# Splitting weights two tiles at a time, and the keys of two heads in one step

## The chip, the cores and the metric

One NeuronCore of a Trainium2 chip runs the whole program. The metric is the device time of one execution in microseconds (us), the median of several runs. Its engines are TensorE (PE, with its weight loads listed as PEld), VectorE (DVE), ScalarE (ACT), GpSimd (POOL) and SyncE (SP), which here only issues DMAs. Each engine works through its own queue in order; semaphores order them among each other.

## What is computed

Three stages follow each other on 4 batches of 576 tokens (2304 in all):

```python
scores = 0.125 * q @ k.T                       # 8 heads of 64, per batch
kth    = 32nd largest score of each row
attn   = softmax(where(scores >= kth, scores, -1e9))
x = (attn @ v), heads side by side             # 2304 x 512
h = x @ w_in                                   # 512 x 2048
y = where(h > 0, h, exp(min(h, 0)) - 1) @ w_out   # 2048 x 512
z = ((y @ w1) * (y @ w2)) @ w3 @ w_out2        # 512 x 1024 twice, 1024 x 1024, 1024 x 512
```

Inputs are float32 in the reference. The kernel gets the weights as 64-bit words.

## The kernel before

**Number formats.** Float32 precision is reached on fast matmuls by splitting each operand into a high half and a low half: a float16 tile `hi` holds the rounded value, `lo` the rest, and a product is hi\*hi + hi\*lo + lo\*hi (three matmuls). Both halves of a weight tile lie in one 128x512 float32 slot: `hi(t)` is its first 512 float16 columns, `lo(t)` the last 512. The weights are 48 such tiles: `Win`, `Wout` and `W12` with 16 each; `W34`, with 8 more, holds the product w3 @ w4, computed on the chip.

**Weight preparation.** For each of w_in, w_out, w1 and w2, `load64` (line 616) loads a 512 KB block of 64-bit words and merges the two 32-bit halves into a float32 tile (L633 ACT, L634 DVE, L635 ACT, L636 POOL). These staged tiles don't have slots of their own: `home` (line 643) places staged tile i in the final slot of tile i + 4 (w_in, w_out) or i + 2 (w1 and w2, together `w12`), and the last ones in slots of `W34` or in `PP`. When all 16 are there, `norm` finds a scale (Gram matmuls L394, DVE reductions), and `convert` (line 655) splits tile by tile: it writes `hi(W[i])` and `lo(W[i])` over the slot in which an earlier staged tile lay. So tile i can be split only after tile i - 4 (w_in, w_out) or i - 2 (w12).

`convert` takes the high half on ACT (L660, a copy to float16 with the scale as a per-partition operand). The low half is made in one of several modes, given by `PAR["cd"]` and `conv_modes`:

- "S": GpSimd scales the staged tile in place (L669) and subtracts the high half (L670). Six tiles of w_in, six of w_out and eight of w12; those of w12 are the odd tiles.
- "D": DVE does both in one instruction (L663). The eight even tiles of w12.
- "P": PE multiplies the staged tile by a scaled identity and subtracts the high half (L675, L676) into a psY bank, and DVE copies the bank out (L679). Ten tiles each of w_in and w_out.

**Keys.** `att_loads` (line 439) loads the keys of one batch and one pair of heads when they are first needed, 16 times in all. For each of the two heads, one DMA fills one of two raw buffers (a ring of two, shared with the values), ACT copies 128x576 to the rounded form (L450), and GpSimd replaces partitions 64 to 127 by the rest (L451). Keys needed again later come back from DRAM.

**Attention.** A step is 128 query rows of two heads: query split (L510 ACT, L511 POOL), QK into the bank psS (L529), evacuation by ACT (L531), eight-at-a-time top-32 on DVE (MAX8 L539, MATCH_REPLACE8 L541, four rounds per head), masking and exponential (L554, L556 ACT), split (L564 ACT, L565 POOL), transposing DMA, the product with the values (L582), normalization on DVE and split (L602 ACT, L603 POOL), and a transposing DMA (L604) into the chunk's activations X. A chunk is 256 tokens, 8 steps; there are nine.

**The rest of a chunk** on PE: units A (x @ w_in, L841 to L843), O (@ w_out, L878 to L880), B (@ w1 and @ w2, L920 to L922) and D (@ W34, L955 to L957), with the evacuations between them on ACT, DVE and GpSimd.

**Order of work.** Nothing is issued in program order. Each operation is recorded with an engine, an estimated cost, the keys it reads and writes and a priority; `Program.emit` (line 232) then simulates the queues forward and backward with these costs and issues the operations in the resulting order, which is fixed from then on. The priority holds an offset from the table `OFF` per kind of work and engine, and a term for the length of the chain behind the operation.

The lines that the change touches most directly:

```python
op("ACT", 613, lambda: A.activation(hi(W[i]), st, AF.Copy, scale=s), [*skeys, sk], [(nm, i)], pr)      # L660
op("POOL", 660, lambda: G.tensor_scalar(st, st, s, 1.0, op0=OP.mult, op1=OP.mult), [sk], skeys, pr)    # L669
op("POOL", 1160, lambda: G.tensor_tensor(lo(W[i]), st, hi(W[i]), op=OP.subtract), ...)                 # L670
```

Of the kernel before, what the change touches and what calls it, by code (L numbers as in the profile page):

```python
# [32 lines left out]
PAR = dict(rings=(2, 3, 4, 3, 1, 2, 5, 3), nxs=3, nxf=2, nxt=3, slack=1.6, fb=2, snake=1, blag=0, hv={}, lv={'wi': 16, 'wo': 16}, whole=(), cd={'wi': [0, 0, 6], 'wo': [0, 0, 6], 'w34': [0, 0, 8], 'w12': [8, 0, 8]}, pv=-577.81, pi=702.591, p34=-453.754, po=123.714, p12=822.408,   # L33
# [5 lines left out]
OFF = {":DVE": 16163, "A0:ACT": -38685, "A0:DVE": -4543, "A0:PE": 21441, "A0:POOL": 23849, "A1:ACT": 1589, "A1:PE": -13628, "A1:POOL": -11110,  # L39
# [214 lines left out]
def kernel(ctx: ExitStack, tc: tile.TileContext, qd, kd, vd, vn, w_in, w_out, w1, w2, w3t, w4, out,  # L254
                                   chunks=CHUNKS):
    nc = tc.nc
    w_in, w_out, w1, w2, w3t, w4 = [a.bitcast(I32) for a in (w_in, w_out, w1, w2, w3t, w4)]
    P = Program()
    CONV = {k: conv_modes(8 if k == "w34" else 16, *v) for k, v in PAR["cd"].items()}
    op = P.op  # L260
    NTL = sum(chunks)

# [11 lines left out]
    def slots(name, n):  # L274
        t = pool.tile([128, n, 512], F32, name=name)
        return t, [t[:, i] for i in range(n)]

    _, Win = slots("win", 16)
    WoutT, Wout = slots("wout", 16)
    W12T, W12 = slots("w12", 16)  # L280
    W34T, W34 = slots("w34", 8)
# [435 lines left out]
    def prep_in(pr):  # L717
        P.tag = "w_in"
        st = []
# [372 lines left out]
```

## Time and profile before

| | us |
|---|---|
| median of 3 runs (lowest to highest) | 1037.14 (1036.56 to 1039.12) |
| the profiled execution, its own time | 1037.07 |
| its span in the profile | 1035.3 |
| PE busy in the span | 955.4 |
| DVE busy | 870.8 |
| ACT busy | 819.4 |
| POOL busy | 739.7 |

Busy time counts the instructions of an engine, without its waits. Instructions of one engine overlap at their ends: an instruction begins before the one ahead of it has ended, so the spacing of starts is shorter than a duration. In the views, an instruction is named by its line, its engine, its operation and output<-input by the program's names; w is a tile of `W12` or `W34`, win and wout those of `Win` and `Wout`.

### The profile page before, as it was taken

Reading aid. Unit: us, or ns where it says so; the run is one execution under the profiler, and the core shown is the slowest. Engines: PE = TensorE matmul, PEld = TensorE weight load, DVE = VectorE, ACT = ScalarE, POOL = GpSimd, SP = SyncE. Lnnn points to the kernel's source line nnn. Section 1 sums busy time; section 2 is a strip of 40 time slices with the busy share of each in tenths; the row PEclk is TensorE's granted clock in tenths of the full one; section 3 lists DMA queues with packets and bytes.
Section 4 is the critical chain, followed back from the end, with each engine's and each line's share of the span. In section 5 each row is a group of like instructions: output and inputs, shape, how many; then the busy total and the mean of one; then the engine's idle time right before and its main releaser. Section 6 shows DMA issues by size and latency. Waiting matters only on the chain.

```text
span 1035.3 us, 24518 instructions
## 1 busy us (share of the span) xinstructions
PE 955.4 (92%) x9096; PEld 770.4 (74%) x9096; DVE 870.8 (84%) x1941; ACT 819.4 (79%) x1517; POOL 739.7 (71%) x795
## 2 busy tenths in 40 slices
PE   2466999896899999999999999999999999999998
PEld 2333455796788878878878897788789889878875
DVE  6999999999999999997999999575999999951010
ACT  6999977998999977976987798587778878944512
POOL 6999966799999846965985597479368657944701
PEclk9897999999999999999999999999999999999999
DMA  9987995867456774555476354524553353330000
GB/s 366 329 273 232 276 251 122 232 197 154 135 126 160 169 137 86 121 136 148 127 175 155 86 121 116 146 57 136 124 132 69 70 114 82 57 91 14 1 22 21
DMA packets 246744, 144.04 MB, mean 139 GB/s; under 512 B 195680, under 2 KB 222304, under 8 KB 246624
## 3 DMA queue, kind: packets, MB, share of 16 engines
q1 hardware_dynamic: 246624, 142.48, 54.1%
q8 instruction: 71, 1.16, 0.5%
q14 instruction: 49, 0.40, 0.1%
HBM read 80.65 MB, written 14.59 MB: 92 GB/s over the span
## 4 chain that ended last, share of the span: by engine, by line
DVE 36%; PE 26%; ACT 15%; POOL 7%; issue 7%; DMA 6%; DVEq 0%; POOLq 0%; ACTq 0%
DVE m L539 16%; DVE wk L541 14%; PE psY L783 3%; PE psR L920 2%; PE psR L921 2%; PE psR L922 2%; DMA pt<-pi 2%; PE psS L529 2%; DMA pp<-w 2%; PE psA L582 2%; ACT s L554 1%; PE psR L841 1%; PE psR L842 1%; PE psR L843 1%; ACT s L531 1%
## 5 line engine op out<-in xcount | busy, mean ns | idle before, releaser
L539 DVE MAX8 m<-wk 128x8 f32<-128x576 f32 x432 | 312.2, 747 | 0.8
L565 POOL TENSOR_TENSOR pi<-s,pi 128x576 f16<-128x576 f32 x144 | 185.5, 1296 | 78.8 <-ACT pi L564 67.7
L541 DVE MATCH_REPLACE8 wk<-m,wk 128x576 f32<-128x576 f32 x288 | 212.5, 741 | 0.0
L920 PE MATMUL psR<-x,w 128*128 128x256 f16 x576 | 157.3, 273 | 3.7 <-DVE t L940 3.7
L841 PE MATMUL psR<-x,win 128*128 128x256 f16 x576 | 157.8, 274 | 0.8 <-DVE t L940 0.5
L843 PE MATMUL psR<-x,win 128*128 128x256 f16 x576 | 157.4, 273 | 0.0
L842 PE MATMUL psR<-x,win 128*128 128x256 f16 x576 | 157.4, 273 | 0.0
L922 PE MATMUL psR<-x,w 128*128 128x256 f16 x576 | 157.0, 273 | 0.5 <-POOL w L670 0.5
L878 PE MATMUL psY<-g,wout 128*128 128x256 f16 x576 | 157.3, 273 | 0.0
L880 PE MATMUL psY<-g,wout 128*128 128x256 f16 x576 | 157.0, 273 | 0.0
L879 PE MATMUL psY<-g,wout 128*128 128x256 f16 x576 | 157.0, 273 | 0.0
L921 PE MATMUL psR<-x,w 128*128 128x256 f16 x576 | 157.0, 273 | 0.0
L554 ACT ACTIVATE s<-s,m 128x576 f32<-128x576 f32 x144 | 110.3, 776 | 40.8 <-DVE m L539 39.2
L529 PE MATMUL psS<-kt,qh 128*128 128x288 f32 x320 | 112.4, 366 | 31.4 <-ACT s L531 24.9
L531 ACT ACTIVATE s<-psS 128x576 f32<-128x576 f32 (+1 forms) x160 | 103.1, 644 | 17.0 <-PE psS L529 11.2
L556 ACT ACTIVATE s<-s,ty 128x576 f32<-128x576 f32 x144 | 107.4, 771 | 3.8 <-POOL ty L550 3.7
L539 DVE MAX8 m<-s 128x8 f32<-128x576 f32 x144 | 106.1, 746 | 3.9 <-ACT s L531 3.4
L541 DVE MATCH_REPLACE8 wk<-m,s 128x576 f32<-128x576 f32 x144 | 106.3, 741 | 0.0
L564 ACT ACTIVATE pi<-s 128x576 f16<-128x576 f32 x144 | 96.5, 679 | 9.4 <-DMA pt<-pi 9.1
L529 PEld LDWEIGHTS psS<-kt,qh 128*128 128x128 f32 x320 | 62.3, 195 | 44.9 <-ACT s L531 20.0
L529 PE MATMUL psS<-kt,ql 128*128 128x288 f32 x320 | 91.5, 300 | 1.0 <-POOL ql L511 1.0
L582 PEld LDWEIGHTS <-pt 128*128 128x128 f16 (+1 forms) x2240 | 77.8, 101 | 17.7 <-issue 8.0
(168 smaller groups left out, 2393.4 us busy)
## 6 DMA issues: line engine op xcount, KB each, us to landing
qr<-qd SPq DMA_DIRECT2D x72, 128.0 KB, 2.7
raw<-kd SPq DMA_DIRECT2D x32, 288.0 KB, 3.3
w<-w_in SPq DMA_DIRECT2D x16, 512.0 KB, 7.5
w<-w_out SPq DMA_DIRECT2D x16, 512.0 KB, 6.0
w<-w3t SPq DMA_DIRECT2D x16, 512.0 KB, 4.8
kd<-kt SPq DMA_DIRECT2D x12, 576.0 KB, 4.0
kt<-kd SPq DMA_DIRECT2D x12, 576.0 KB, 3.9
w<-w SPq DMA_DIRECT2D x12, 512.0 KB, 4.7
```

The lines of the kernel that those rows point to most:

```text
L529: T.matmul(psS[:, half, 0:288], lhsT=L[qs][:, hh], rhs=KT[kk][:, hh, half * 288:half * 288 + 288], start=li == 0, stop=li == 1)
L539: op("DVE", 665, lambda r=r, src=src, m8=m8, hh=hh: V.max(m8[:, hh, 8 * r:8 * r + 8], src), [skey], [mk], p1 + PAR["ot"] * STEP)
L541: op("DVE", 727, lambda r=r, src=src, w=w, m8=m8, hh=hh: V.match_replace(w, m8[:, hh, 8 * r:8 * r + 8], src, -3.0e38), [skey, mk], [k], p1 ...
L565: op("POOL", 1240, lambda Y=Y, PIs=PIs, hh=hh: G.tensor_tensor(PIs[:, hh, S:2 * S], Y[:, hh], PIs[:, hh, 0:S], op=OP.subtract), hks, [pk], ...
L841: T.matmul(o, lhsT=hi(W)[:, cs], rhs=X[:, 0, kd_, 0:N], start=kd_ == 0, stop=False)
L842: T.matmul(o, lhsT=hi(W)[:, cs], rhs=X[:, 1, kd_, 0:N], start=False, stop=False)
L843: T.matmul(o, lhsT=lo(W)[:, cs], rhs=X[:, 0, kd_, 0:N], start=False, stop=kd_ == 3)
L878: T.matmul(o, lhsT=hi(W)[:, cs], rhs=rh, start=ft == 0 and m % 2 == 0, stop=False, skip_group_check=True)
L879: T.matmul(o, lhsT=hi(W)[:, cs], rhs=rl, start=False, stop=False, skip_group_check=True)
L920: T.matmul(o, lhsT=hi(W)[:, cs], rhs=X[:, 0, kd_, 0:N], start=kd_ == 0, stop=False)
L921: T.matmul(o, lhsT=hi(W)[:, cs], rhs=X[:, 1, kd_, 0:N], start=False, stop=False)
L922: T.matmul(o, lhsT=lo(W)[:, cs], rhs=X[:, 0, kd_, 0:N], start=False, stop=kd_ == 3)
```

## The change

The high halves of w_in, w_out, w1 and w2 are made for two neighbouring tiles by one ACT instruction of 128x(2x512). Where the pair's mode is "S", one GpSimd instruction scales both tiles and one subtracts both. Modes "P" and "D" still work tile by tile, after the common high half. Modes are given per pair now, with the same number of tiles in each: w_in and w_out have three "S" pairs and five "P" pairs each, w12 four "D" pairs and four "S" pairs in turn. For keys, both raw buffers are loaded, then one ACT instruction copies both heads and one GpSimd instruction subtracts both. The estimated costs follow. All entries of `OFF` have new values.

```diff
-PAR = dict(... cd={'wi': [0, 0, 6], 'wo': [0, 0, 6], 'w34': [0, 0, 8], 'w12': [8, 0, 8]}, ...
+PAR = dict(... cd={'wi': [0, 0, 3], 'wo': [0, 0, 3], 'w34': [0, 0, 8], 'w12': [4, 0, 4]}, ...
-OFF = {":DVE": 16163, "A0:ACT": -38685, "A0:DVE": -4543, "A0:PE": 21441, "A0:POOL": 23849, "A1:ACT": 1589, ...
+OFF = {":DVE": 17176, "A0:ACT": -44777, "A0:DVE": -8789, "A0:PE": 18968, "A0:POOL": 19901, "A1:ACT": -5916, ...
...
-    CONV = {k: conv_modes(8 if k == "w34" else 16, *v) for k, v in PAR["cd"].items()}
+    CONV = {k: conv_modes(8, *v) for k, v in PAR["cd"].items()}
...
         for hh in range(2):
-            rs = nxt("raw", 2)
-            kr = raw[rs][:, 0:S]
-            dma(kr, kd[b, 2 * p + hh], 128 * S * 4, [], [("raw", rs)], pr)
-            op("ACT", 574, lambda kr=kr, hh=hh: A.activation(KT[ks][:, hh], kr, AF.Copy), [("raw", rs)], [("k", ks)], pr)
-            op("POOL", 1370, lambda kr=kr, hh=hh: G.tensor_tensor(KT[ks][64:128, hh], kr[64:128], KT[ks][64:128, hh].bitcast(F32), op=OP.subtract),
-               [("raw", rs)], [("k", ks)], pr)
+            dma(raw[nxt("raw", 2)][:, 0:S], kd[b, 2 * p + hh], 128 * S * 4, [], [("raw", hh)], pr)
+        rks, kr = [("raw", 0), ("raw", 1)], RAWT[:, :, 0:S]
+        op("ACT", 66 + 508 * 2, lambda: A.activation(KT[ks], kr, AF.Copy), rks, [("k", ks)], pr)
+        op("POOL", 143 + 1220 * 2, lambda: G.tensor_tensor(KT[ks][64:128], kr[64:128], KT[ks][64:128].bitcast(F32), op=OP.subtract), rks, [("k", ks)], pr)
...
+    def pair(WT, nm, i):
+
+        k = len(HOMES[nm])
+        if i < 16 - k:
+            return WT[:, i + k:i + k + 2]
+        return PP[:, 4:8].rearrange("p (a c) b -> p a (c b)", a=2) if nm == "w12" else W34T[:, i - 12 + 4 * (nm == "wo"):][:, 0:2]
+
+    def convert2(W, WT, nm, i, st, s, sk, pr, sid, kind="y"):
+
+        d2, ks = pair(WT, nm, i), [st[i][1], st[i + 1][1]]
+        keys = ks[0] + ks[1]
+        f2 = WT[:, i:i + 2].bitcast(F16)
+        h2, l2 = f2[:, :, 0:512], f2[:, :, 512:1024]
+        op("ACT", 66 + 547 * 2, lambda: A.activation(h2, d2, AF.Copy, scale=s), [*keys, sk], [(nm, i), (nm, i + 1)], pr)
+        if CONV[nm][i // 2] == "S":
+            op("POOL", 86 + 574 * 2, lambda: G.tensor_scalar(d2, d2, s, 1.0, op0=OP.mult, op1=OP.mult), [sk], keys, pr)
+            op("POOL", 80 + 1045 * 2, lambda: G.tensor_tensor(l2, d2, h2, op=OP.subtract), [*keys, (nm, i), (nm, i + 1)], [(nm, i, "l"), (nm, i + 1, "l")], pr)
+            return
+        for h in range(2):
+            rest(W, nm, i + h, st[i + h][0], ks[h], s, sk, pr, sid, kind, CONV[nm][i // 2])
+
     def convert(W, nm, i, st, skeys, s, sk, pr, sid, kind="y"):
...
-        mode = CONV[nm][i]
+        rest(W, nm, i, st, skeys, s, sk, pr, sid, kind, CONV[nm][i])
+
+    def rest(W, nm, i, st, skeys, s, sk, pr, sid, kind, mode):
...
-        for i in range(16):
+        for i in range(0, 16, 2):
             P.tag = "w_in.c"
-            convert(Win, "wi", i, st[i][0], st[i][1], scal("sin"), ("sc", "ni"), pr + PAR["ci"] * STEP, 0)
+            convert2(Win, WinT, "wi", i, st, scal("sin"), ("sc", "ni"), pr + PAR["ci"] * STEP, 0)
...
-        return [lambda i=i: convert(W12, "w12", i, st[i][0], st[i][1], scal(("s1", "s2")[i // 4 % 2]), ("sc", ("n1", "n2")[i // 4 % 2]), pr + PAR["c12"] * STEP, i // 4 % 2 * 2, "rot")
-                for i in range(16)]
+        return [lambda i=i: convert2(W12, W12T, "w12", i, st, scal(("s1", "s2")[i // 4 % 2]), ("sc", ("n1", "n2")[i // 4 % 2]), pr + PAR["c12"] * STEP, i // 4 % 2 * 2, "rot")
+                for i in range(0, 16, 2)]
```

`prep_out` changes as `prep_in` does. `rest` holds the modes' code of `convert`, unchanged.

## Rows read from the trace of the kernel before

**Rows 1.** The page's busy table: engine, busy us (share of the span), instructions.
```profile
PE 955.4 (92%) x9096; PEld 770.4 (74%) x9096; DVE 870.8 (84%) x1941; ACT 819.4 (79%) x1517; POOL 739.7 (71%) x795
```

**Rows 2.** Busy time by stage: stretch, length, each engine's busy us (instructions), PE clock, DMA.
```profile
core 0: us, PE busy (x) PEld busy (x) DVE busy (x) ACT busy (x) POOL busy (x), PEclk, DMA share, GB/s
46.00:107.00 61.00, 41.41 (x210) 20.68 (x210) 57.32 (x116) 59.91 (x106) 59.59 (x56) 0.84 0.83 265
107.00:183.00 76.00, 72.97 (x415) 40.49 (x415) 74.14 (x160) 63.63 (x122) 54.13 (x60) 0.98 0.90 213
183.00:243.00 60.00, 54.75 (x584) 48.44 (x581) 58.38 (x137) 56.21 (x103) 53.20 (x53) 0.97 0.83 214
243.00:300.00 57.00, 45.22 (x498) 39.42 (x495) 55.34 (x131) 53.03 (x99) 56.26 (x59) 0.97 0.53 127
300.00:912.00 612.00, 605.74 (x6285) 515.45 (x6283) 571.68 (x1280) 505.30 (x953) 440.06 (x490) 1.00 0.51 119
```

**Rows 3.** The timeline of PE at two joints: start us, length us, instructions.
```profile
106.75 0.38 PE L676 MATMUL psY<-wout,nident 128*128 128x512 f16 x1
107.28 1.96 PE L783 MATMUL psY<-w,pp 128*128 128x512 f32 x4
...
183.07 0.27 PE L841 MATMUL psR<-x,win 128*128 128x256 f16 x1
```

**Rows 4.** The activations X from 170 to 184 us: transposing DMAs, first and last start.
```profile
L604 SPq DMA_TRANSPOSE x<-xt x2: 1167/1167/1167, 171.0 to 180.8; - x2
...
DMA to landing us min/median/max: 2.3/3.7/5.1
```

**Rows 5.** The timeline of ACT: start us, length us, instructions (xN: several merged).
```profile
72.21 0.68 ACT L450 ACTIVATE kt<-raw 128x576 fp32r<-128x576 f32 x1
72.78 0.64 ACT L531 ACTIVATE s<-psS 128x576 f32<-128x576 f32 x1
...
85.98 2.54 ACT L660 ACTIVATE wout<-wout,sc 128x512 f16<-128x512 f32 x4
```

**Rows 6.** ACT copies by line: duration ns min/median/max, first to last start us.
```profile
L602 ACT ACTIVATE xt<-xf x72: 292/306/348, 85.2 to 940.3; 128x128 f16<-128x128 f32 x72
...
L450 ACT ACTIVATE kt<-raw x32: 665/682/741, 4.1 to 720.4; 128x576 fp32r<-128x576 f32 x32
...
L660 ACT ACTIVATE w<-w,sc x21: 705/712/742, 225.2 to 320.6; 128x512 f16<-128x512 f32 x21
```

**Rows 7.** High halves (L660 alone) in the two stages: ACT busy us (instructions).
```profile
46.00:107.00 61.00, 20.91 (x31) 0.84 0.83 265
243.00:300.00 57.00, 13.85 (x20) 0.97 0.53 127
```

**Rows 8.** The timeline of GpSimd, as rows 5.
```profile
88.11 2.28 POOL L670 TENSOR_TENSOR wout<-wout 128x512 f16<-128x512 f32 x2
...
94.76 1.41 POOL L451 TENSOR_TENSOR kt<-raw,kt 64x576 fp32r<-64x576 f32 x1
96.25 1.29 POOL L636 TENSOR_TENSOR w<-w 128x512 int32<-128x512 int32 x1
```

**Rows 9.** GpSimd instructions by line, as rows 6.
```profile
L603 POOL TENSOR_TENSOR xt<-xf,xt x72: 416/429/1013, 120.4 to 941.4; 128x128 f16<-128x128 f32 x72
...
L669 POOL TENSOR_SCALAR w<-w,sc x16: 684/692/1126, 103.7 to 332.5; 128x512 f32<-128x512 f32 x16
...
L670 POOL TENSOR_TENSOR w<-w x14: 1152/1159/1618, 245.0 to 333.3; 128x512 f16<-128x512 f32 x14
```

**Rows 10.** GpSimd's subtractions for weights (L670 alone) in the two stages, as rows 7.
```profile
46.00:107.00 61.00, 12.02 (x10) 0.84 0.83 265
243.00:300.00 57.00, 15.40 (x13) 0.97 0.53 127
```

**Rows 11.** GpSimd's subtractions for keys (L451 alone) in the two stages, as rows 7.
```profile
46.00:107.00 61.00, 7.05 (x5) 0.84 0.83 265
243.00:300.00 57.00, 6.00 (x4) 0.97 0.53 127
```

**Rows 12.** Waits of PE, 243 to 300 us: in total, times, longest.
```profile
PE psS L529 <- ACT s L531: 7.5, 5, 2.8
```

**Rows 13.** DVE instructions with two SBUF inputs by line, as rows 6.
```profile
L663 DVE SCALAR_TENSOR_TENSOR w<-w,sc x7: 725/761/1198, 245.8 to 279.6; 128x512 f16<-128x512 f32 x7
...
L477 DVE SCALAR_TENSOR_TENSOR vv<-raw,sc,vv x16: 870/1412/1933, 38.2 to 710.9; 128x640 f16<-128x640 f32 x16
```

**Rows 14.** High halves of w12 and the last subtraction: first and last start us.
```profile
L660 ACT ACTIVATE w<-w,sc x17: 705/711/742, 242.9 to 278.3; 128x512 f16<-128x512 f32 x17
...
L670 POOL TENSOR_TENSOR w<-pp,w x1: 1163/1163/1163, 285.5 to 285.5; 128x512 f16<-128x512 f32 x1
```

More of the change, by code (lines that the diff above doesn't have):

```diff
@@ L31 @@
 FLAT = 2.0 ** -100
-PAR = dict(rings=(2, 3, 4, 3, 1, 2, 5, 3), nxs=3, nxf=2, nxt=3, slack=1.6, fb=2, snake=1, blag=0, hv={}, lv={'wi': 16, 'wo': 16}, whole=(), cd={'wi': [0, 0, 6], 'wo': [0, 0, 6], 'w34': [0, 0, 8], 'w12': [8, 0, 8]}, pv=-577.81, pi=702.591, p34=-453.754, po=123.714, p12=822.408,
+PAR = dict(rings=(2, 3, 4, 3, 1, 2, 5, 3), nxs=3, nxf=2, nxt=3, slack=1.6, fb=2, snake=1, blag=0, hv={}, lv={'wi': 16, 'wo': 16}, whole=(), cd={'wi': [0, 0, 3], 'wo': [0, 0, 3], 'w34': [0, 0, 8], 'w12': [4, 0, 4]}, pv=-577.81, pi=702.591, p34=-453.754, po=123.714, p12=822.408,
            pis=-107.607, pos=19.797, p12s=-197.302, p34s=838.328, ci=825.351, co=-921.962, cos=928.659, c12=388.003, m34=497.922, c34=2463.442,
@@ L37 @@
            pvb=-3829.627, lag1=-475.176, lagb=401.111)
-OFF = {":DVE": 16163, "A0:ACT": -38685, "A0:DVE": -4543, "A0:PE": 21441, "A0:POOL": 23849, "A1:ACT": 1589, "A1:PE": -13628, "A1:POOL": -11110,
[35 rows of a table removed]
-       "att8x:SP": 2116, "attsa:ACT": -38945, "attsa:PE": -45630, "attsk:ACT": -46655, "attsk:POOL": -12175, "attsk:SP": -20106, "attsm:ACT": 59355,
-       "attsm:POOL": 27934, "attsp:ACT": -27773, "attsp:POOL": 4475, "attsp:SP": 12804, "attsq:ACT": -29254, "attsq:POOL": 26261, "attsq:SP": -8330,
-       "attss:ACT": -10714, "attss:PE": -9165, "attst:DVE": 53351, "attsv:ACT": 18840, "attsv:DVE": 15311, "attsv:SP": 12330, "attsx:ACT": 11365,
[3 rows of a table removed]
-       -8612, "w_in.c:ACT": 800, "w_in.c:DVE": 9028, "w_in.c:PE": -11799, "w_in.c:POOL": -7583, "w_in.n:DVE": 24888, "w_in.n:PE": 9694, "w_in:ACT":
-       -220, "w_in:DVE": -7426, "w_in:POOL": -33659, "w_in:SP": -55119, "w_out.c:ACT": 5219, "w_out.c:DVE": -531, "w_out.c:PE": -22400,
-       "w_out.c:POOL": -5233, "w_out.n:DVE": -38749, "w_out.n:PE": 8892, "w_out:ACT": 14086, "w_out:DVE": 35892, "w_out:POOL": 23776, "w_out:SP":
-       23054, "w_v0:DVE": -70692, "w_v0:PE": -2179, "w_v0:SP": -19017, "w_v1:DVE": -12335, "w_v1:PE": 38647, "w_v1:SP": 59851, "w_v:DVE": -36828}
@@ new lines @@
+OFF = {":DVE": 17176, "A0:ACT": -44777, "A0:DVE": -8789, "A0:PE": 18968, "A0:POOL": 19901, "A1:ACT": -5916, "A1:PE": -14322, "A1:POOL": -13852,
[35 rows of a table added]
+       "att8x:SP": 2774, "attsa:ACT": -38362, "attsa:PE": -41090, "attsk:ACT": -53721, "attsk:POOL": -21219, "attsk:SP": -24187, "attsm:ACT": 61598,
+       "attsm:POOL": 30700, "attsp:ACT": -19918, "attsp:POOL": 12140, "attsp:SP": 20215, "attsq:ACT": -29379, "attsq:POOL": 27916, "attsq:SP": -4825,
+       "attss:ACT": -13089, "attss:PE": -13726, "attst:DVE": 56075, "attsv:ACT": 30412, "attsv:DVE": 15763, "attsv:SP": 14219, "attsx:ACT": 8030,
[3 rows of a table added]
+       "w_in.c:ACT": -2911, "w_in.c:DVE": 2946, "w_in.c:PE": -22203, "w_in.c:POOL": -15865, "w_in.n:DVE": 30855, "w_in.n:PE": 12851, "w_in:ACT": 1202,
+       "w_in:DVE": -8936, "w_in:POOL": -43254, "w_in:SP": -51586, "w_out.c:ACT": 4297, "w_out.c:DVE": 4017, "w_out.c:PE": -20204, "w_out.c:POOL":
+       -8369, "w_out.n:DVE": -47339, "w_out.n:PE": 6449, "w_out:ACT": 19636, "w_out:DVE": 33601, "w_out:POOL": 33288, "w_out:SP": 27281, "w_v0:DVE":
+       -71540, "w_v0:PE": -7591, "w_v0:SP": -18187, "w_v1:DVE": -1305, "w_v1:PE": 42247, "w_v1:SP": 64316, "w_v:DVE": -48127}
@@ L276, in slots @@
         return t, [t[:, i] for i in range(n)]
-    _, Win = slots("win", 16)
+    WinT, Win = slots("win", 16)
     WoutT, Wout = slots("wout", 16)
@@ L672, in convert, with minus @@
         ps, pk = bank(kind)
-        def rest():
+        def minus():
             T.matmul(ps, lhsT=SI[sid], rhs=st, start=True, stop=False)
             T.matmul(ps, lhsT=nident, rhs=hi(W[i]), start=False, stop=True)
-        op("PE", 1250, rest, [*skeys, (nm, i), ("si", sid), "ident"], [pk], pr)
+        op("PE", 1250, minus, [*skeys, (nm, i), ("si", sid), "ident"], [pk], pr)
         if spread(i, PAR["lv"].get(nm, 0)):
@@ L757, in prep_out @@
         scaled_identity(1, scal("sout"), ("sc", "no"), pr)
-        for i in range(16):
+        for i in range(0, 16, 2):
             P.tag = "w_out.c"
-            convert(Wout, "wo", i, st[i][0], st[i][1], scal("sout"), ("sc", "no"), pr + (PAR["co"] + i * PAR["cos"]) * STEP, 1)
+            convert2(Wout, WoutT, "wo", i, st, scal("sout"), ("sc", "no"), pr + (PAR["co"] + i * PAR["cos"]) * STEP, 1)
     def prep_34(pr):
```

76 rows, old and new, of the table OFF are left out of this document.

## The prediction

> **What bounds the kernel now.** The profiled execution took 1037.07 us, of which the span is 1035.3; the median of the runs shown is 1037.14, so a sum made against this execution needs no correction (0.07 us). A difference under 0.3% (3.1 us) can't be told from no change here.
>
> I read the busy table first: PE is busy 955.4 us, or 92% [rows 1]. A mean over stages says little, so the next view is the busy time by stage [rows 2]. The reader is to see three kinds of stage. From 300 to 912 us PE is busy 605.7 of 612 us: there it is simply full, and cheaper ACT or GpSimd work buys nothing. The same holds from 107 to 183, the float32 product of w3 and w4 (73.0 of 76). Between 46 and 107 us PE is busy only 41.4 of 61 us, and ACT (59.9), GpSimd (59.6) and DVE (57.3) are all nearly full: this is where w_in and w_out are unpacked and split. Between 243 and 300 it is PE 45.2 of 57, GpSimd 56.3, DVE 55.3, ACT 53.0: this is where w1 and w2 are split. The change acts in those two stages.
>
> The timeline of PE gives the joints. The product L783 begins at 107.28, directly after the splits of w_out, and the first A unit (L841) at 183.07 [rows 3]. The second joint has two parents: the last transposed activations of chunk 0 were issued at 180.8 and transfers of that kind take 2.3 to 5.1 us [rows 4]. So a product that ends earlier helps only if attention, which DVE paces, is earlier too.
>
> **The change, part by part.** The durations are not what an instruction costs a full engine; the spacing of starts is. On ACT four splits of 128x512 in a row took 2.54 us, with 0.71 for the last, so they start every 0.61; a key copy begins at 72.21 and the next instruction at 72.78, a spacing of 0.57 [rows 5, 6]. The slope comes from two plain copies, 306 ns for 128 elements and 682 ns for 576, or 0.84 ns per element [rows 6]. So 512 elements are 0.43 of the 0.61 us and 0.18 is a fixed part; for keys 0.57 less 0.48 leaves 0.09. A pair pays the fixed part once.
>
> *High halves.* 24 pairs take the place of 48 instructions, each saving 0.18 us. Between 46 and 107 there are 31 of them, some 15.5 pairs, or 2.8 us; between 243 and 300 twenty [rows 7], of which 16 belong to w1 and w2: 8 pairs, 1.4 us.
>
> *GpSimd's low halves.* Two subtractions in a row took 2.28 us with 1.16 for the second: a spacing of 1.12 [rows 8, 9]. The slope from 128 elements (429 ns) to 512 (1159 ns) is 1.90 ns per element [rows 9], so 1024 should last 2.13 us and, with the same overlap of 0.04, take 2.09: a pair saves 0.15. The scaling before it exists in one length only. Its saving lies between 0 and, by the nearest row, the subtraction's 0.15; I take half, 0.08. A pair then saves 0.23. Ten subtractions lie between 46 and 107, so 5 pairs or 1.15 us; thirteen between 243 and 300 [rows 10], eight of them for w1 and w2, so 4 pairs or 0.9 us. Modes stay as they were in number (6, 6 and 8 tiles on GpSimd, 8 on DVE, 20 through PE), so PE and DVE do the same work.
>
> The GPSIMD Engine Reference of the Trainium skill (section 3.1) speaks against this term: it gives 4497 ns for a two-input add of 2048 elements and calls the cost per element a floor of the read port. A quarter of that is 1.12 us (an estimate from that page), the very spacing seen here, so by it a pair saves nothing on GpSimd and, since GpSimd's 59.6 us would remain in the first stage, the sum below would be 0.3 us instead of 3.1. That is one of the rivals.
>
> *Keys.* Two ACT copies become one (0.09 us saved per pair), two GpSimd subtractions one. These are spaced 1.49 us (94.76 to 96.25) [rows 8], 0.37 more than a subtraction of 512 elements on all partitions. The saving is at least the 0.15 of a subtraction and at most 0.40, if the partition offset or the extra waiting costs once per instruction; I take 0.30. Five lie in the first stage and four in the second [rows 11]: 2.5 and 2 pairs, 0.75 and 0.6 us on GpSimd, 0.2 and 0.2 on ACT. The loads stay 32 DMAs of the same size on SP's queue, but the first raw buffer comes free only with the second, 1.49 us later. What is queued behind it on SP is the load of the values, and behind that query loads and transposes. No row shows this wait; it is worth between 0 and 4.5 x 1.49 = 6.7 us on SP in the two stages. I take 0, because the values are first read one attention step after the keys, and keep the other end for the range.
>
> *Coarser waits.* In w_in and w_out a tile is written over the staged tile four places earlier, so pairs still form two independent chains, and PE's first product of a split reads staged data only. I price this at 0; its cover is the other chain. In w1 and w2 the shift is two tiles, see the rivals.
>
> *The order.* All offsets of the planner are new, so the order on every queue may differ. I have no row for that; it widens the range.
>
> **The sum.** First stage: ACT falls from 59.9 by 3.0 to 56.9 and GpSimd from 59.6 by 1.9 to 57.7; DVE stays at 57.3. GpSimd is now the last, so the stage shrinks by 59.9 - 57.7 = 2.2 us, and not by ACT's 3.0. The product moves forward with it. Second stage: GpSimd falls from 56.3 by 1.5 to 54.8, under DVE's 55.3, so DVE ends it: 0.9 us. Elsewhere PE or DVE is full: 0. Together 3.1 us: 1037.1 - 3.1 = **1034.0 us**. This is the bound itself, so the chance of this case falls half on each side of it.
>
> **Rivals.**
>
> *The savings add up (1029, faster).* In the first stage ACT, PE, DVE and GpSimd hand each tile on, and the three of them wait for each other rather than for one. If each saving shortens the relay, the stage gives 3.0 + 1.9 and the second 1.6 + 1.5, 8.0 together. For it: PE idles 20 us in the first stage while no other engine idles over 4 [rows 2]. Against: DVE gives nothing, and is at 57.3 of 61.
>
> *No gain (1036.8, same).* Either GpSimd saves nothing, so that the first stage shrinks only from ACT's 59.9 to GpSimd's 59.6, or DVE's own work carries chunk 0's activations to 183 and chunk 1's beyond 285, whatever ACT does. For it: DVE is busy 74.1 of 76 and 58.4 of 60 us between the two stages [rows 2]. Against: in the first stage it has 3.7 us of idle time to give.
>
> *The chain of w1 and w2 (1042, slower).* The split of a pair writes its halves over the staged tiles of the pair before, so all eight pairs form one chain, where single tiles had two: DVE's and GpSimd's ran side by side. Now a high half waits in ACT's in-order queue for GpSimd's subtraction of the pair before, and behind it wait the evacuations of the scores, for which PE's QK products already wait 7.5 us in this stage [rows 12]. The bare chain is four DVE pairs of 1.14 + 2 x 0.76 [rows 13] and four GpSimd pairs of 1.14 + 1.3 + 2.1 (the scaling as two of 0.69 less 0.08 [rows 9]), with 0.3 for two hand-offs each: 4 x 3.0 + 4 x 4.8 = 31 us. Now the sixteen tiles take from 242.9 to 286.7, or 43.8 us [rows 14]. The point from which it decides is therefore 12 us of waiting in eight pairs, 1.5 us each, a little over one foreign GpSimd instruction (1.16 us) more per pair on an engine that is busy 56.3 of 57 us. If ACT stands half of the 3.4 us that each of GpSimd's four pairs takes, that is 7 us, less the 2.2 gained before: 1042.
>
> *The shared port (1042, slower).* DVE's two-input subtractions last 725 to 1198 ns for the same shape (L663), and those of the values 870 to 1933 (L477) [rows 13]: something holds them, for up to about the length of one GpSimd subtraction. If this comes from GpSimd, an instruction of twice the length holds twice as long: eight subtractions of w1 and w2 by 1.05 more is 8.4 us on DVE, less 3.1: 1042. Against: with the single chain these eight mostly run while no doubled subtraction of the weights does. The rule behind it stands in SBUF — State Buffer of the Trainium skill, in "Who interferes with whom": a DVE instruction with two SBUF inputs and a GpSimd instruction that reads SBUF exclude each other, for the whole instruction. The spread of these rows agrees with it.
>
> **How the numbers follow.** Forecast 0.42 (0.22 faster, 0.20 same), savings add up 0.19, no gain 0.17, the chain 0.14, the port 0.08. Faster: 0.22 + 0.19 = 0.41; same: 0.20 + 0.17 = 0.37; slower: 0.22. The likeliest is 1034.0. For 8 in 10 the range reaches below 1029 by what a GpSimd pair may save beyond my choice (9 pairs by 0.07, 4.5 by 0.10: 1.1 us) and a little for the order, 1027, and on the other side to 1041.5, just short of the slow rivals and over the 1040.7 that SP's wait would give.
>
> **What would show it.** Right: ACT's high halves at about 1.14 us for 1024 elements, GpSimd's subtractions at 2.13 and keys under 2.8; L783 beginning near 105.1 and L841 near 181; the stage before PE is full ending 3 us earlier; PE's sum unchanged. The chain: w1's and w2's splits spread over more than 44 us, with ACT idle before them for GpSimd, and longer waits of L529 for ACT. The port: DVE's L663 or L477 at over 2 us. No gain: L783 earlier but L841 still near 183. The forecast is wrong altogether if the difference arises after 300 us, where I see nothing to gain: then the new order made it, not the pairs.

## The result, and the profile after

The changed kernel takes 1046.37 us (median of 6 runs, 1045.00 to 1053.94) against 1039.46 us for the kernel before, run beside it (median of 6). The ratio is 1.0091, with a 95% interval of 1.0062 to 1.0119: it is slower by about 9 us, outside the range of the prediction (1027 to 1041.5). Two of the six runs, 1052.79 and 1053.94, weigh in the ratio; the medians alone are 6.9 us apart. The execution profiled is the slowest of the six, 1053.94 us with a span of 1052.2, so its trace shows 17 us of difference where the medians show 7.

The page's busy table of the changed kernel answers to [rows 1].

```profile
PE 962.1 (91%) x9096; PEld 774.1 (74%) x9096; DVE 876.1 (83%) x1941; ACT 817.5 (78%) x1477; POOL 733.4 (70%) x759
```

The joins did what they were meant to: 40 instructions fewer on ACT, 36 on GpSimd, and less busy time on both. The joined instructions, by line (columns as in [rows 6, 9]; L666 makes a pair of high halves, L668 scales and L669 subtracts a pair, L449 and L450 copy and subtract the keys of two heads):

```profile
L666 ACT ACTIVATE w<-w,sc x7: 1132/1149/1170, 255.2 to 296.1; 128x1024 f16<-128x1024 f32 x7
L668 POOL TENSOR_SCALAR win<-win,sc x3: 1108/1113/1122, 49.8 to 64.2; 128x1024 f32<-128x1024 f32 x3
L669 POOL TENSOR_TENSOR win<-win x3: 2127/2133/2136, 51.0 to 66.0; 128x1024 f16<-128x1024 f32 x3
L669 POOL TENSOR_TENSOR w<-pp,w x1: 2142/2142/2142, 302.9 to 302.9; 128x1024 f16<-128x1024 f32 x1
L449 ACT ACTIVATE kt<-raw x16: 1148/1162/1190, 5.2 to 734.7; 128x1152 fp32r<-128x1152 f32 x16
L450 POOL TENSOR_TENSOR kt<-raw,kt x16: 2612/2634/2657, 6.5 to 736.5; 64x1152 fp32r<-64x1152 f32 x16
```

So the loss is not in what a joined instruction costs. The busy time by stage (columns as in [rows 2]) shows where it is. First the kernel before, in two stretches that [rows 2] don't hold:

```profile
26.00:46.00 20.00, 8.38 (x75) 7.21 (x73) 19.97 (x47) 18.40 (x33) 17.80 (x15) 0.90 0.92 315
300.00:1035.30 735.30, 725.07 (x7302) 608.73 (x7299) 588.55 (x1324) 550.03 (x1030) 481.79 (x533) 1.00 0.44 103
```

The changed kernel:

```profile
26.00:46.00 20.00, 10.77 (x76) 9.07 (x76) 14.38 (x31) 18.95 (x34) 17.42 (x14) 0.73 1.06 379
46.00:107.00 61.00, 36.70 (x193) 20.05 (x193) 60.07 (x123) 55.05 (x85) 57.08 (x44) 0.72 0.78 240
107.00:183.00 76.00, 66.92 (x344) 35.02 (x345) 70.40 (x148) 61.75 (x115) 50.65 (x53) 0.98 0.87 207
243.00:300.00 57.00, 44.80 (x485) 39.09 (x483) 56.49 (x121) 49.84 (x86) 53.06 (x51) 0.88 0.60 138
300.00:1052.20 752.20, 741.40 (x7460) 623.10 (x7459) 600.79 (x1358) 564.40 (x1042) 494.54 (x534) 1.00 0.45 103
```

The last row of each is the one to read. From 300 us on PE is full and its clock is full in both, so the time is what PE still has to do: 741.4 against 725.1 us, 16.3 of the 16.9 us by which the spans differ. The whole loss is work that PE had not done by 300 us. Part of it is time in which PE stood and part is its clock: for the same 9096 matmuls PE is busy 962.1 us instead of 955.4, at a granted clock of 0.89 instead of 0.94 before 300 us, so of the 16.9 us some 6.7 are longer matmuls and 10.2 idle time. Before 300 us DVE, which paces attention, is idle 5.6 us from 26 to 46 (it was full) and 5.6 from 107 to 183 (1.9 before). The product starts 12.2 us later and A 13.4 later than in [rows 3] (PE's timeline):

```profile
119.48 1.96 PE L805 MATMUL psY<-w,pp 128*128 128x512 f32 x4
...
196.48 0.27 PE L863 MATMUL psR<-x,win 128*128 128x256 f16 x1
```

DVE's timeline shows what its first idle time is (start, length, instruction, idle time before it and who ended it):

```profile
29.20 0.67 DVE L632 SCALAR_TENSOR_TENSOR w<-w,psR 128x512 int32<-128x512 int32 x1
30.89 0.69 DVE L632 SCALAR_TENSOR_TENSOR w<-w,psR 128x512 int32<-128x512 int32 x1 [1.02 <-ACT psR L631]
32.59 0.69 DVE L632 SCALAR_TENSOR_TENSOR w<-w,psR 128x512 int32<-128x512 int32 x1 [1.01 <-ACT psR L631]
34.66 0.69 DVE L632 SCALAR_TENSOR_TENSOR w<-w,psR 128x512 int32<-128x512 int32 x1 [1.38 <-ACT psR L631]
```

Four merges of weight words stand next to each other in DVE's queue, with no step of attention between them, and three of them wait for ACT. None of the changed lines is in these rows. The groups of DVE from 26 to 46 us (busy us, mean ns of one, idle time before), first before, then after:

```profile
L634 DVE SCALAR_TENSOR_TENSOR w<-w,psR 128x512 int32<-128x512 int32 x11 | 7.3, 673 | 0.0
L539 DVE MAX8 m<-wk 128x8 f32<-128x576 f32 x6 | 4.5, 752 | 0.0
```
```profile
L632 DVE SCALAR_TENSOR_TENSOR w<-w,psR 128x512 int32<-128x512 int32 x11 | 7.5, 684 | 3.6 <-ACT psR L631 3.6
...
L537 DVE MAX8 m<-wk 128x8 f32<-128x576 f32 x2 | 1.5, 756 | 0.0
```

Both do eleven merges, but before six of attention's later MAX8 stand among them, after two. This is a matter of order, and the order is new. That it sets the time is not shown by these rows; the experiments ask that.

### The profile page after: what moved, and what is told of

Same layout as the page of the kernel before. It is cut to its first block, busy times and chain, and to the rows that moved or that the text cites. A ratio compares the mean times of both kernels' runs of the same rounds, so it can differ in the third digit from the quotient of the medians.

```text
span 1052.2 us, 24373 instructions
## 1 busy us (share of the span) xinstructions
PE 962.1 (91%) x9096; PEld 774.1 (74%) x9096; DVE 876.1 (83%) x1941; ACT 817.5 (78%) x1477; POOL 733.4 (70%) x759
## 4 chain that ended last, share of the span: by engine, by line
PE 35%; DVE 33%; ACT 8%; DMA 8%; issue 4%; POOL 4%; SPq 0%; DVEq 0%; ACTq 0%; POOLq 0%
DVE m L537 15%; DVE wk L539 13%; PE psR L942 4%; PE psR L943 4%; PE psR L944 4%; DMA pt<-pi 3%; PE psS L527 2%; PE psA L580 2%; PE psR L863 2%; PE psY L805 2%; PE psR L865 2%; PE psR L864 2%; DMA pp<-w 2%; PE psY L900 2%; PE psY L901 2%
```

## Experiments

Two theories. **Order**: the joined instructions save about what was forecast, and the new order of all queues costs more. **Coarse pairs**: the joins cost by themselves, because a pair waits for two inputs and releases two outputs late, or because its instructions are long. All ratios are to the kernel before, run beside each kernel. The last two columns are from the profiled execution: PE's busy time after 300 us, and DVE's in the 20 us from 26 to 46. The ratio is made over all runs, so it differs a little from that of the medians. In fourteen of the twenty rows the profiled time is PE's time after 300 us plus 310 to 314, so that column carries the result; in the others (e2 and e4 to e8) PE also idles after 300.

| kernel | median us | ratio (95%) | profiled us | PE after 300 | DVE 26-46 |
|---|---|---|---|---|---|
| before | 1039.46 | | 1037.07 | 725.1 | 20.0 |
| the change | 1046.37 | 1.0091 (1.0062 to 1.0119) | 1053.94 | 741.4 | 14.4 |
| e1 its order, all single | 1052.63 | 1.0139 (1.0121 to 1.0157) | 1052.33 | 740.0 | 14.3 |
| e2 old order, keys joined | 1070.47 | 1.0304 (1.0287 to 1.0320) | 1071.52 | 741.6 | 20.0 |
| e3 old order, high halves | 1043.65 | 1.0038 (1.0023 to 1.0053) | 1041.12 | 728.7 | 20.0 |
| e4 old order, both | 1074.09 | 1.0337 (1.0320 to 1.0354) | 1072.34 | 742.9 | 20.0 |
| e5 as e2, second place | 1067.78 | 1.0294 (1.0278 to 1.0310) | 1070.78 | 745.8 | 19.9 |
| e6 as e3, second place | 1065.89 | 1.0261 (1.0233 to 1.0289) | 1066.06 | 749.9 | 20.0 |
| e7 before, new offsets | 1053.52 | 1.0154 (1.0137 to 1.0171) | 1051.01 | 734.9 | 15.7 |
| e8 the change, old offsets | 1069.50 | 1.0309 (1.0294 to 1.0325) | 1070.34 | 751.2 | 15.1 |
| e9 keys, remade order | 1035.45 | 0.9959 (0.9942 to 0.9975) | 1036.64 | 725.7 | 20.0 |
| e10 keys and high halves, remade | 1046.38 | 1.0062 (1.0041 to 1.0083) | 1046.96 | 734.3 | 19.9 |
| e11 some of both, remade | 1037.97 | 0.9995 (0.9978 to 1.0012) | 1038.44 | 726.8 | 19.8 |
| e12 before, remade | 1040.52 | 1.0021 (1.0006 to 1.0036) | 1038.39 | 724.6 | 20.0 |
| e13 order of e9, all single | 1036.79 | 0.9970 (0.9956 to 0.9984) | 1037.82 | 727.7 | 20.0 |
| e14 keys, w_in and w_out, remade | 1043.29 | 1.0035 (1.0017 to 1.0054) | 1039.52 | 727.3 | 19.9 |
| e15 keys, w1 and w2, remade | 1036.07 | 0.9966 (0.9950 to 0.9982) | 1036.09 | 724.6 | 20.0 |
| e16 the change, its order remade | 1044.42 | 1.0061 (1.0037 to 1.0085) | 1044.36 | 732.1 | 14.5 |
| e17 modes by pairs, remade | 1041.40 | 1.0020 (1.0002 to 1.0039) | 1040.98 | 727.8 | 19.6 |
| e18 the change, from the old order | 1037.92 | 1.0001 (0.9981 to 1.0022) | 1041.63 | 728.8 | 19.9 |

**The joins taken back at the order of the change (e1).** Every pair is issued as two instructions, back to back:

```diff
-        op("ACT", 66 + 547 * 2, lambda: A.activation(h2, d2, AF.Copy, scale=s), [*keys, sk], [(nm, i), (nm, i + 1)], pr)
+        op("ACT", 66 + 547 * 2, lambda: [A.activation(h2[:, e], d2[:, e], AF.Copy, scale=s) for e in range(2)], [*keys, sk], [(nm, i), (nm, i + 1)], pr)
```

GpSimd's scaling and subtraction and both steps of the keys likewise.

> The changed kernel, its order of work kept word for word, but each pair is issued as two instructions of one tile (one head) back to back. Theory 'order': joining saves engine time as its durations show and the new order costs more; then undoing the joins here makes the time worse or leaves it: 0 to 8 us over the changed kernel's 1046.4, so 1046 to 1054, a ratio of 1.007 to 1.014 to the kernel before. Rival 'long instructions' (waits held up by an instruction of twice the length, DVE held by GpSimd's long subtractions): with short instructions the loss goes away at the same order: 1036 to 1042, a ratio of 0.997 to 1.003.

Busy time of the high halves before 300 us (stretch, length, busy us (instructions), then PE clock, DMA share and GB/s), the changed kernel first:

```profile
0.00:300.00 300.00, 26.34 (x23) 0.89 0.79 222
```
```profile
0.00:300.00 300.00, 30.61 (x46) 0.89 0.78 222
```

A pair saves (30.61 - 26.34) / 23 = 0.19 us. Without the joins the kernel is not faster but slower: 1.0139 against 1.0091, or 0.0048, some 5 us, with 1.5 to 8.5 if the two intervals are independent. So at this order the joins gain, as forecast, and the loss is elsewhere: that long instructions make it falls. The two singles stand at one place and still wait for both inputs, so what the waits of a pair cost is not asked here.

**The joins put into the order of the kernel before (e2 to e6).** The joined instruction stands at the place of the first of the two (e5, e6: of the second); what depends on it moves behind it, all else stays.

```diff
+JOIN_KEYS, JOIN_HIGH = True, False
...
+                P.join(("kh", b, p), lambda: A.activation(KT[ks], RAWT[:, :, 0:S], AF.Copy))
...
-        for i in sorted(self.joins, key=pos.get):
+        for i in sorted(self.joins, key=pos.get, reverse=True):
```

e3 has False, True and e4 True, True; the last two lines are the step to e5 and e6.

> The kernel before with its own order; only the keys of both heads are joined, one ACT copy and one GpSimd subtraction at the place of the first, after both loads. Theory 'order': 16 GpSimd pairs that save 0.19 us each and ACT pairs 0.1 to 0.2, less the wait of the first copy for the second load, most of it only in the first 10 us: 1035 to 1042 beside 1039.5, a ratio of 0.996 to 1.003. Rival 'coarser hand-offs': the first QK starts 2.8 us later as in the changed kernel, and the raw buffers stay taken longer in each load: 1042 to 1048, a ratio of 1.003 to 1.008.

> The kernel before with its own order and offsets; only the high halves of w_in, w_out, w1 and w2 are joined in pairs on ACT (24 instructions of 128x1024 take the place of 48). GpSimd's halves stay single. Theory 'order': ACT saves 0.2 to 0.28 us per pair, some 5 to 6 us of its time, of which the path gets 0 to 3: 1036 to 1040, a ratio of 0.997 to 1.000. Rival 'coarser hand-offs': a pair waits for two staged tiles and releases two tiles late, which the fixed order was not made for: 1042 to 1050, a ratio of 1.003 to 1.010.

> The kernel before with its own order; keys and high halves joined, the sum of the two kernels sent beside this one. Theory 'order': 1033 to 1041, a ratio of 0.994 to 1.002, so that a version better than both may stand here. Rival 'coarser hand-offs': the two losses add up, 1045 to 1055, a ratio of 1.006 to 1.015.

> As the kernel with joined keys at the place of the first head (1070.5), but the joined ACT copy and the joined GpSimd subtraction stand at the place of the second head's. There ACT waited 32.9 us for second loads, with scores and splits queued behind it. Theory 'blocked queue' (the loss is the fixed order's: the copy stands where the second load can't have landed): the wait falls below 10 us and most of the 31 us comes back: 1038 to 1046, a ratio of 0.999 to 1.007. Rival 'coarse keys' (both raw buffers are held for both heads, QK gets its keys later wherever the copy stands): 1055 to 1072, a ratio of 1.015 to 1.032.

> As the kernel with joined high halves at the place of the first tile (1043.7), but at the place of the second. The low half of the first tile then waits one instruction longer. Theory 'blocked queue': a pair no longer waits in ACT's queue for its second staged tile, 1037 to 1041, a ratio of 0.998 to 1.002. Rival 'coarser hand-offs': GpSimd, PE and DVE wait for the first tile's high half instead, and the loss of 4 us stays or grows: 1043 to 1050, a ratio of 1.003 to 1.010.

The keys cost 31 us, far beyond both expectations. The waits point to a cause that I had not named: the queues are worked off in order, and a joined copy stands in front of ready work until its second load is there. Waits of the kernel before and of e2 (engine, instruction <- what it waited for: us in total, times, longest; L485 and L489 are the joined copy and subtraction):

```profile
ACT kt L450 <- DMA raw<-kd: 7.1, 7, 4.3
...
SPq L347 <- POOL kt L451: 30.0, 18, 4.1
```
```profile
ACT kt L485 <- DMA raw<-kd: 32.9, 12, 5.9
...
SPq L380 <- POOL kt L489: 53.6, 11, 8.5
```

ACT stands 32.9 us in front of second loads, with ready work behind it, and SP waits 53.6 instead of 30.0 us for a raw buffer. In e5 that wait of ACT falls to 1.0 us, as "blocked queue" had it, but ACT now waits for the loads of the values, which are late in turn:

```profile
DVE vv L514 <- ACT vv L511: 30.8, 8, 7.7
...
ACT vv L511 <- DMA raw<-vd: 22.3, 6, 5.7
```

The time did not come back: 1.0294 lies in the range of the rival, "coarse keys", and moving one instruction is not enough. e4 is e2 and e3 added up. High halves cost 4 us at the first place, as "coarser hand-offs" had it, and 27 at the second, beyond both expectations. In e6 PE stands 8.9 us before 300 us for late high halves of w_in, 8.5 of them at once; in e3 it never waits more than 0.4 us for a high half. What the rest of the 27 is, is open. So far a join costs up to 31 us in an order made for single instructions, and gains 5 in one made for joins.

**Only the table (e7, e8).** `OFF` of one kernel in the other.

> The kernel before in all its instructions, single tiles and single heads, with the changed kernel's table of offsets: another order and nothing else. Theory 'order': the early stage gets worse as in the changed kernel, product from 107 to 115 or later, 1045 to 1060, a ratio of 1.005 to 1.020. Rival 'joins' (the new table costs nothing by itself): 1036 to 1042, a ratio of 0.997 to 1.003.

> The changed kernel in all its instructions, with the table of offsets of the kernel before. Theory 'order': neither table is good or bad by itself, each fits only the graph of operations that it was found for; here the joined graph with the old table: 1050 to 1075, a ratio of 1.010 to 1.035, slower than the change with its own. Rival 'bad table' (the new table is the cause): near or under the kernel before, 1033 to 1042, a ratio of 0.994 to 1.003.

With no instruction changed, the new table costs 1.54%, 16 us. With the old table the change costs 3.1%. Neither table is the cause alone: each goes with its own set of operations, which is what "order" expected. DVE's idle time from 26 to 46 is there in both.

**The order made anew (e9 to e13).** The order is written into the kernel as a list. It was found by starting from the order of the kernel before and changing places at random, keeping what doesn't lengthen the program's own estimate (an estimate, no time of the chip).

```diff
-        for _, i in order:
-            self.ops[i][2]()
+        for i in seq:
+            (self.joins[i][1] if i in self.joins else self.ops[i][2])()
```

> The same instructions as the two kernels with joined keys (1070.5 and 1067.8), but the whole order is made anew for the joined instructions, starting from the order of the kernel before, and written into the kernel as a list. Theory 'order': the 30 us were the price of an order made for other instructions; here ACT and SP no longer wait for keys in front of ready work: 1033 to 1041, a ratio of 0.995 to 1.003. Rival 'coarse keys' (two raw buffers held for both heads cost the time in any order): 1055 to 1072, a ratio of 1.016 to 1.033.

> Keys and all 24 pairs of high halves joined (1074.1 at the order of before), the order made anew in the same way. Theory 'order': 1035 to 1045, a ratio of 0.997 to 1.006, near or under the changed kernel's 1046.4. Rival 'coarse pairs': the weights' pairs cost by themselves, above 1046, a ratio over 1.008.

> Keys of six loads and nine pairs of high halves joined, chosen by the estimated costs, the others single; the order made anew. Theory 'order': 1030 to 1038, a ratio of 0.992 to 1.000, so that this one can be faster than both kernels. Rival 'coarse pairs': slower than before, 1042 and over.

> The control of the three beside it: nothing joined, the instructions of the kernel before, the order made anew in the same way. If the remaking itself gives the gain, this one is as fast as the best of the three, 1032 to 1039, a ratio of 0.994 to 1.001. If joins add a gain to it, this one is slower than they are by 1 to 8 us. If such a remade order is worse on the chip than its estimated costs say, all four lie over 1042.

> The kernel with joined keys and a remade order (1035.5), that order kept, but each joined copy and subtraction is issued as two of one head, back to back. If the joined instructions give the gain: 16 subtractions of 0.2 to 0.4 us and 16 copies of 0.1 to 0.2, some 5 to 8 us of engine time, of which the stages before PE is full hold half: 1037 to 1042, a ratio of 0.999 to 1.003. If the order gives it: as with joined keys, 1034 to 1037, a ratio of 0.995 to 0.998. If a joined instruction delays its first half's readers by more than it saves: under 1034.

The joined keys that cost 31 us now gain 4. ACT waits for their loads no longer than before, though SP still waits longer:

```profile
ACT kt L562 <- DMA raw<-kd: 6.2, 6, 1.7
...
SPq L457 <- POOL kt L566: 41.9, 13, 5.3
```

e9 is faster than both kernels, by 0.4%. But e13, with the same order and single instructions, can't be told from it: by the ratios the instructions give 1.1 of the 4 us (-1 to 3.4 if the intervals are independent), and the order the rest. e12, the control with nothing joined, is no faster than before: it is this order that is good, not the remaking. e11 lies between the two (0.9995). e10 (1.0062) decides nothing: it lies over the range of "order" (to 1.006) and under that of "coarse pairs" (over 1.008), with the median of the change. All the high halves took 11 us more than the keys alone, in an order remade for them.

**Which pairs (e14 to e16).** The joins chosen by weight; e16 is the change with a list made from its own order.

> Keys and the 16 pairs of high halves of w_in and w_out joined, those of w1 and w2 single, order remade. If the single chain of w1 and w2 carries the loss: 1033 to 1038, a ratio of 0.995 to 0.999. If the pairs of w_in and w_out carry it (PE's first product of a split and GpSimd wait for two staged tiles in the stage in which all are nearly full): 1041 to 1047, a ratio of 1.003 to 1.009.

> Keys and the 8 pairs of high halves of w1 and w2 joined, those of w_in and w_out single, order remade. If the single chain of w1 and w2 carries the loss: 1041 to 1047, a ratio of 1.003 to 1.009, with their splits spread over more than 50 us. If the pairs of w_in and w_out carry it: 1033 to 1038, a ratio of 0.995 to 0.999.

> The changed kernel with all its instructions; its order is remade from its own order in the same way and written in as a list. Theory 'order': some of the 8 us come back, 1038 to 1044, a ratio of 1.000 to 1.006. Rival 'coarse pairs' (no order helps): 1045 to 1050, a ratio over 1.006.

The pairs of w1 and w2 cost nothing (0.9966), those of w_in and w_out go with 1.0035, a difference of 0.0069, 7 us. e16 gives back 3 us of the 9, which the intervals don't separate from none, and keeps DVE's gap at the start (14.5). The gap alone doesn't set the time: e10 is without it and as slow (1.0062). Until here "coarse pairs" still held for w_in and w_out.

**The modes, and the whole change from the old order (e17, e18).** e17 takes from the change only the layout of the modes; e18 has all of its instructions.

```diff
-        mode = CONV[nm][i]
+        mode = MODES[nm][i // 2] if PAIRED and nm != "w34" else CONV[nm][i]
...
+                    P.join((nm, e, "s"), lambda: G.tensor_scalar(d2, d2, s, 1.0, op0=OP.mult, op1=OP.mult))
...
+                P.join((nm, e, "d"), lambda: G.tensor_tensor(l2, d2, h2, op=OP.subtract))
```

> The kernel before with single instructions throughout, but the modes of the low halves laid out by pairs as in the change (for w_in and w_out three neighbouring pairs on GpSimd, five through PE; for w1 and w2 pairs in turn on DVE and GpSimd), the order remade from that of before. If the layout costs nothing: 1034 to 1041, a ratio of 0.996 to 1.002, like the control with nothing changed (1040.5). If two neighbouring tiles on one engine in a row hold up the chain of slots: 1042 to 1048, a ratio of 1.003 to 1.009.

> All instructions of the changed kernel, in an order that is remade starting from the order of the kernel before. Theory 'order' (a better order for the joined instructions was there to be had): 1033 to 1041, a ratio of 0.995 to 1.002. Rival 'coarse pairs' (the pairs of w_in and w_out cost in any order): 1042 to 1050, a ratio of 1.003 to 1.011, with the product at 109 us or later, as in the other kernels with these pairs (109.1 to 116.6).

The layout costs nothing that can be told: e17 is at 1.0020, the control e12 at 1.0021. e18 settles what the order is worth. The change with all its pairs, in an order that starts from that of the kernel before, is as fast as the kernel before: 1.0001 against 1.0091 in its own order, 0.0090 or 9 us, 5.6 to 13 if independent (7.6 by the medians). The busy time by stage of e18:

```profile
26.00:46.00 20.00, 7.07 (x68) 6.25 (x68) 19.90 (x49) 19.92 (x34) 18.00 (x16) 0.95 0.90 325
46.00:107.00 61.00, 38.80 (x224) 22.75 (x224) 57.28 (x110) 55.98 (x90) 56.71 (x44) 0.74 0.85 256
107.00:183.00 76.00, 70.17 (x324) 36.08 (x325) 76.00 (x160) 61.49 (x111) 51.77 (x53) 1.00 0.82 209
243.00:300.00 57.00, 51.82 (x581) 45.61 (x580) 55.52 (x138) 51.63 (x91) 50.95 (x48) 0.94 0.68 151
300.00:1072.00 772.00, 728.81 (x7328) 611.36 (x7326) 595.13 (x1331) 554.97 (x1029) 488.74 (x533) 1.00 0.42 98
```

DVE is full again from 26 to 46 and from 107 to 183, and PE has 728.8 us left at 300. Another explanation falls with it. The product starts at 121.7 in e18, later than in the change, so its start doesn't set the end:

```profile
L917 PE MATMUL psY<-w,pp x128: 590/592/697, 121.7 to 187.1; 128*128 128x512 f32 x128
```

PE's granted clock belongs to the loss, and it goes with the order: over the span it is 0.964 to 0.974 in the six runs of the change and 0.978 to 0.984 in the ten of e18, with the same instructions. From 46 to 107 us it is 0.74, as low as the 0.72 of the change, so that stage's clock doesn't make the difference; but it is 0.95 instead of 0.73 from 26 to 46 and 0.94 instead of 0.88 from 243 to 300. In e18 PE is busy 959.0 us in all, so of the 12.3 us between the two profiled spans 3.1 go with the longer matmuls and 9.2 with idle time. Which places in the order do it is not shown.

## Why the prediction was wrong

**The step that failed** is "The order. All offsets of the planner are new, so the order on every queue may differ. I have no row for that; it widens the range." I priced the order at 0, and the range reached 1041.5 for other reasons. It measured 9 us on the change (e18 against the change) and 16 us on the unchanged instructions (e7), larger than the sum of all other terms. The rows could have warned me: where three engines are 94 to 98% busy [rows 2], little room is left to catch up when a queue stands a few us. No row bounded a replaced order from either side, so it needed a chance of its own as a rival, and got none.

**Unit costs: right, with one size off.** High half of a pair 1.14 us forecast, 1.13 to 1.17 measured (medians by tile); the saving 0.18, measured 0.19. GpSimd's subtraction 2.13 forecast, 2.133 measured. Before 300 us, e1 against the change, it saved (20.54 - 19.22) / 9 = 0.15 per pair, as forecast; the scaling (12.87 - 10.64) / 9 = 0.25, over my bound of 0.15; the keys (16.78 - 15.82) / 6 = 0.16 on GpSimd, where I took 0.30 of 0.15 to 0.40. The spacing of 1.49 us behind that bound is longer than the subtraction's own 1.41 [rows 8], so GpSimd stood idle in it. By the 4497 ns that the GPSIMD Engine Reference of the Trainium skill (section 3.1) gives for 2048 elements, 1024 would take 2.25 us (an estimate), and I read its cost per element as no saving, though it names a dispatch per instruction without a figure; the trace has 2.13 and a saving, and decides.

**The sum: not refuted.** I forecast 3.1 us; the joins at one order gave 5 (1.5 to 8.5). e18 against e17, the same modes in two remade orders, gives 0.0019, 2 us (-1 to 5), and e9 against e13, the keys alone, 1.1; that speaks against the 8.0 of "the savings add up", which the first doesn't exclude, though the two orders of e17 and e18 differ.

**SP's wait at 0, coarser waits at 0: right only in some orders.** In the old order the keys cost 31 us and the high halves 4. In the order of e9 the joined keys cost nothing against single ones (e13), and in e18 all pairs together cost nothing; in the remade order of e10 the high halves still cost 11. In the change itself SP's loads wait 50.7 us for the keys' subtraction, where it was 30.0 before and is 27.4 in e18:

```profile
SPq L347 <- POOL kt L450: 50.7, 12, 8.1
```

My 6.7 us was no bound: I counted SP's own wait, not what ACT and DVE hold back while they wait for what SP brings late.

**"PE's sum unchanged"** was a sign of being right, and failed: 962.1 against 955.4 us, at the lower clock. I had no term for that.

**"The product moves forward with it"** was wrong as a link: e18 has a later product than the change and ends 12.3 us earlier by the profiled runs (1041.63 against 1053.94). What counts is all that PE has done by 300 us.

**The rivals.** *The chain of w1 and w2*: its mark came, splits over 50 us, from 255.2 to 302.9 + 2.14 = 305.0. PE's waits for the evacuation of the scores, which were to grow, did not (5.9 us from 243 to 300, against 7.5 before), and the cost is not the chain's: in e18 the same chain takes from 248.8 to 291.6, 43 us like the single tiles before, and e15, whose high halves of w1 and w2 are joined too, is faster than before. *The shared port*: its mark came too, L475 with 4.32 us and L685 with up to 2.48. But with single instructions they reach 4.67 and 2.51 (e1), so doubled instructions don't lengthen the hold, and undoing them gained nothing. The eight low halves of w1 and w2 on DVE took 6.95 us in all before, 10.19 in the change, 10.01 with singles (e1) and 7.12 in e18, so the longer holds go with the order. *No gain*: its first reason, GpSimd saving nothing, fell with the durations above. Its second, that DVE's own work sets the joints whatever ACT does, is open: e1 shows a gain in the order of the change, but e18 against e17 and e9 against e13 exclude neither no gain at all nor 3.1 us.

**"Wrong altogether if the difference arises after 300 us"** named the new order but put it in the wrong place: the difference arose before 300, where I looked for the gain.

**Left open.** Whether pairs in w_in and w_out cost a few us in a good order: with keys and these pairs e14 is at 1.0035, with everything e18 is at 1.0001, and each is one order out of many. Separate raw buffers for the values might take the keys' waits away by themselves; that wasn't tried.

## What to carry to other kernels

When a change touches a kernel whose queues are filled by a planner, take it as two changes and time them apart: the old instructions in the new order, and the new instructions issued singly in it. Joining instructions saved a few us here, about as the spacing of rows said, and a new order cost 9 to 16. Before believing a gain from joins, look at what stands behind the joined instruction in its in-order queue when its second input is late.

## What the runs showed of the hardware that was not expected

A DVE instruction with two SBUF inputs was held much longer than one GpSimd instruction lasts. L475 of the changed kernel by its durations (columns as in [rows 13]), then the longest one in DVE's timeline, and GpSimd's timeline beside it:

```profile
L475 DVE SCALAR_TENSOR_TENSOR vv<-raw,sc,vv x16: 862/924/4323, 35.9 to 725.3; 128x640 f16<-128x640 f32 x16
```
```profile
67.00 4.32 DVE L475 SCALAR_TENSOR_TENSOR vv<-raw,sc,vv 128x640 f16<-128x640 f32 x1
```
```profile
65.97 2.13 POOL L669 TENSOR_TENSOR win<-win 128x1024 f16<-128x1024 f32 x1
68.06 2.51 POOL L634 TENSOR_TENSOR wout<-wout,w 128x512 int32<-128x512 int32 x2
70.54 0.84 POOL L548 TENSOR_TENSOR ty<-m 128x2 f32<-128x2 f32 x1
```

The shortest lasts 0.86 us, so this one stood for about 3.5, through a subtraction and two merges that GpSimd ran without a gap. The small instruction behind them lasted 0.84 us here and 0.20 in the median of its 72, so by then DVE had its turn and GpSimd waited. With single instructions it is the same: one of 4.67 us in e1, behind two subtractions and two merges; in e18 one lasted 5.20. SBUF — State Buffer of the Trainium skill ("Who interferes with whom") has a DVE instruction with two SBUF inputs and a GpSimd instruction that reads SBUF contend for a port pair that is locked for one of them. The trace agrees, and adds that several GpSimd instructions in a row can go first.

Also unexpected: joining two of GpSimd's scalings saves more than joining two of its subtractions (0.25 against 0.15 us per pair, e1 against the change).
